# Decoded weights summed in PSUM on TensorE, and gl moved to VectorE, in an attention and two-MoE kernel

## The chip, the cores and the metric

The kernel runs on one core of one Trainium2 chip. The metric is the device time of one execution in microseconds; the time of the kernel before is the median of three runs.

## What is computed

Packed attention feeds a dense MLP, and that feeds a mixture of eight experts, of which each token takes two. Cut to what matters here:

```python
p_packed = sm_attn(p, k, v)              # 32 packed queries per head over 576 keys
x = sm_attn(q, p_packed, p_packed)       # 4608 tokens x 512
h = x @ w_in                             # 512 -> 2048
g = np.maximum(h, 0.0) ** 2
x = g @ w_out                            # 2048 -> 512
# then: noisy top-2 gate, and per expert relu(x @ w1[e]) @ w2[e], weighted and added up
```

The weights `w_in` and `w_out` are float32 to NumPy's eye, but this kernel's inputs arrive as 64-bit words (the host only views their bits), so the chip has to turn pairs of 32-bit words into float32 first. That is the decoding of which this document speaks.

## The kernel before

The kernel has two stages. In the first, the 4608 tokens go through the dense MLP in 16 blocks of 288 (block j). In the second, the eight experts each take three tiles of gathered tokens. Blocks 0 to 14 and all that they need are *units*: each unit has an engine, a cost, a list of units that must come first, and the PSUM buffers that it takes. A planner in `schedule()` simulates the engines in the order of time and emits the units in one fixed order, by priorities (`AHEAD`, in thousands of ns per kind of unit) and due times (`DUE`). Engines then run their queues strictly in that order. Block 15 and the experts are emitted by a loop written out by hand behind it.

The units are these.

- **Decoding** (`decode(n)`, 32 chunks of 128 x 512: 16 of `w_in`, 16 of `w_out`, alternating). A load; o0 on ScalarE (L206); o1 to o5 on VectorE (L210, L214, L218, L222, L226), which leave a high part in `dec_a` and a small part in `dec_t`; o6 on GpSimd adds the two (L235 into `win`, L232 into `dec_a` for `w_out`). For `w_out` ScalarE rounds the sum to fp32r as the high half of `wo` (o7, L104 by the helper `act_copy`), and VectorE subtracts it for the low half (o8, L241).
- **Part 1** (`part1(n)`, kind A): scores of packed queries (L291), softmax, transposes (L310, L312), products with v (L324), for a half of a batch's heads; two of them fill `pk[b]`.
- **Preparation** (`prepare(b, q)`, kind P): `pk[b]` times a quarter of `win` (L374), which folds `p_packed` into `w_in`; ScalarE and VectorE split the result into high and low halves in `ring` (L395).
- **Part 2** (`part2(j)`, kind Q): scores of block j's tokens against `pk`, softmax, transposed; ScalarE rounds it to `xT[j, 0]` and the difference goes to `xT[j, 1]` (L449; VectorE for blocks 0 and 1, `JA = 2`, else GpSimd).
- **MLP steps** (`moe_step(j, f)`, kind M, f from 0 to 15): six first-layer matmuls (`moe_l1`, L648) into `ph`; ScalarE's relu (L655) and square; `gh` is the rounded square and `gl` the rest (`moe_gl`, L671; VectorE for blocks 0 and 1, else GpSimd, after VectorE's square at L666); then twelve second-layer matmuls (`moe_l2`, L680) into four accumulators. Step f needs chunk f of `w_out` decoded; steps run in one chain through all blocks.
- **Routing** (`logits`, `route`, kinds R and U): gates of finished blocks, top 2, ranks, and scatters of list entries to `lst` in DRAM by GpSimd (L620), each behind the one before.

PSUM has two buffers tagged `side` (`side()`), which part 1, part 2, the preparations and the routing share. Filler matmuls on `ones` (L1103) keep TensorE going in gaps before 45 us (`WARM`). In block 15's first step the loop loads the list of the first expert and computes a group index from it on VectorE (`group_index`, L790), and the copies of block 14's accumulators to `x2T` (`moe_x2`, L687) come behind it.

Products keep close to fp32 accuracy by splitting both factors into two fp32r halves; three of the four cross terms are multiplied (`TERMS`).

Of the kernel before, what the change touches and what calls it, by code (L numbers as in the profile page):

```python
# [9 lines left out]
F = mybir.dt.float32  # L10
# [11 lines left out]
P = 128  # L22
# [20 lines left out]
for x, sl in enumerate((1, 2, 3, 4, 5, 6, 7, 9, 11, 12, 13, 14, 15, 16)):  # L43
    G0.setdefault(sl, []).append((x // 8, x % 8 // 2, 2 * (x % 2)))
QB, PKB = 2, 2
STB = 3
# [9 lines left out]
FULL = 1275  # L56
AHEAD = {"r": 38.7, "d": 21, "D": 10.3, "a": 17.1, "A": 59.2, "q": 41.7, "Q": 4.8, "p": 44.4, "P": 6.5, "R": 18.2, "M": 1.4, "w": 0.2}
DUE = 13
RING = 8
# [26 lines left out]
def program(ctx, tc, qT, kT, v, pT, w_in, w_out, wg, wn, noise, w1, w2, out):  # L86
# [86 lines left out]
    p1, c_p1 = open_pool("p1", "left")  # L173

    chunks = []
    for i in range(NFF + 4):
# [20 lines left out]
    def decode(n):  # L197
# [26 lines left out]
        def o5():  # L224
            a, t = st["a"].bitcast(F), st["t"].bitcast(F)
            nc.vector.scalar_tensor_tensor(t, raw[n][:, :, 0].bitcast(U32), 2.0 ** -52, t,  # L226
                                           op0=OP.mult, op1=OP.mult)

        def o6():
            a, t = st["a"].bitcast(F), st["t"].bitcast(F)  # L230
            if kind:
                nc.gpsimd.tensor_add(a, a, t)  # L232
            else:
                a, t = (y.rearrange("p (c f) -> p c f", c=4) for y in (a, t))
                nc.gpsimd.tensor_add(win[:, :, P * i:P * i + P], a, t)  # L235

# [3 lines left out]
        def o8():  # L240
            nc.vector.tensor_sub(wo[:, i, 1], st["a"].bitcast(F), wo[:, i, 0].bitcast(F))  # L241

        x = ("d", n)
        unit(("r", n), "sp", load, [("d", n - STB, 5)], dma=524288)
        unit(x + (0,), "act", o0, [("r", n), ("d", n - 2, 6)], 520)
        unit(x + (1,), "dve", o1, [x + (0,)], 480)
        unit(x + (2,), "dve", o2, [x + (1,)], 600)
        unit(x + (3,), "dve", o3, [x + (2,), ("d", n - TB, 6), ("d", n - TB, 8)], 950)
        unit(x + (4,), "dve", o4, [x + (3,)], 680)
        unit(x + (5,), "dve", o5, [x + (4,)], 680)  # L250
        unit(x + (6,), "pool", o6, [x + (5,)] + (lent if not kind and i >= LENT_FROM else []), 1400)
        if kind:
            unit(x + (7,), "act", o7, [x + (6,)], 600)
            unit(x + (8,), "dve", o8, [x + (7,)], 690)

# [121 lines left out]
    def prepare(b, q):  # L377
        n = 8 * b + 2 * q
        st = {}

        def u_g():
            st["m"] = [side(f"mp{r}", [P, 512]) for r in range(2)]
            heads(b, st["m"], win[:, :, 512 * q:512 * q + 512])

        def half(a, r):
            return ring[:, entry(n):entry(n) + 2, a, 256 * r:256 * r + 256]

        def u_h():
            wm[b, 2 * q], wm[b, 2 * q + 1] = piece(n), piece(n + 1)
            for r in range(2):  # L390
                act_copy(half(0, r), st["m"][r].rearrange("p (n f) -> p n f", n=2))

        def u_l():
            for r in range(2):
                nc.vector.tensor_sub(half(1, r), st["m"][r].rearrange("p (n f) -> p n f", n=2), half(0, r).bitcast(F))  # L395

        x = ("P", b, q)
        m = n - RING + 1
        old = [("M", 2 * (m // 8) + 1, 2 * (m % 8) + 1, "1")] if m >= 0 else []
        unit(x + ("g",), "pe", u_g, [("A", 2 * b, "y"), ("A", 2 * b + 1, "y")] +  # L400
             [("d", chunks.index((0, 4 * q + i)), 6) for i in range(4)] + old, 900, psum=(x + ("l",),) * 2)
        unit(x + ("h",), "act", u_h, [x + ("g",)], 1200)
        unit(x + ("l",), "dve", u_l, [x + ("h",)], 1240)
# [3 lines left out]
    def part2(j):  # L407
# [40 lines left out]
        def u_d():  # L448
            (nc.vector if j < JA else nc.gpsimd).tensor_sub(xT[j, 1], st["aT"], xT[j, 0].bitcast(F))  # L449

# [8 lines left out]
        unit(x + ("h",), "act", u_h, [x + ("t",), ("M", j - 2, NFF - 1, "1")], 620)  # L459
        unit(x + ("d",), "dve" if j < JA else "pool", u_d, [x + ("h",)], 700 if j < JA else 1600)  # L460

# [190 lines left out]
    def moe_g(j, f):  # L652
# [3 lines left out]
        gh = mo.tile([P, BLK], FR, name="gh", bufs=3)  # L656
        if j < JA:
            nc.scalar.activation(g, g, AF.Square)
# [3 lines left out]
        gs[j, f] = g, gh  # L662

    def moe_gg(j, f):
        g = gs[j, f][0]
        nc.vector.tensor_mul(g, g, g)  # L666

    def moe_gl(j, f):
        g, gh = gs[j, f]
        gl = mo.tile([P, BLK], FR, name="gl", bufs=3)  # L670
        (nc.vector if j < JA else nc.gpsimd).tensor_sub(gl, g, gh.bitcast(F))  # L671
        gs[j, f] = gh, gl
# [29 lines left out]
    def moe_step(j, f):  # L702
# [6 lines left out]
        if j < JA:  # L709
            unit(x + ("l",), "dve", lambda: moe_gl(j, f), [x + ("g",)], 400)  # L710
        else:
            unit(x + ("q",), "dve", lambda: moe_gg(j, f), [x + ("g",)], 400)
            unit(x + ("l",), "pool", lambda: moe_gl(j, f), [x + ("q",)], 850)
        if (j, f) in ((NS - 1, NFF - 1), (NS - 1, NFF - 2)):
# [194 lines left out]
    def schedule():  # L909
# [20 lines left out]
        def kind(x):  # L930
            if x[0] == "d" and x[-1] in (7, 8):
                return "w"
            if x[0] == "d":
# [375 lines left out]
```

## Time and profile before

| | |
|---|---|
| median of 3 runs | 1748.86 us (1743.95 to 1750.26) |
| the profiled execution | 1746.33 us, of which the span 1744.5 us |
| mean granted TensorE clock | 0.972 |
| TensorE busy | 1643.3 us (94%) |
| VectorE busy | 839.5 us (48%) |
| ScalarE busy | 616.2 us (35%) |
| GpSimd busy | 762.2 us (44%) |

The profile comes from one execution. Engines: PE is TensorE's matmuls, PEld its weight loads, DVE VectorE, ACT ScalarE, POOL GpSimd, SP the queue that issues most transfers. A line number is that of the kernel before; a copy by ScalarE stands at L104, the helper's line, so it is told apart by its tiles. In a window, "busy" is the time covered by at least one instruction; records of a group may overlap. PEclk is the granted TensorE clock as a share of full speed: 1.00 is 2.4 GHz and 0.50 is 1.2 GHz. In brackets behind an instruction stands the idle time before it and what ended it.

### The profile page before, as it was taken

Reading aid. Unit: us, or ns where it says so; the run is one execution under the profiler, and the core shown is the slowest. Engines: PE = TensorE matmul, PEld = TensorE weight load, DVE = VectorE, ACT = ScalarE, POOL = GpSimd, SP = SyncE. Lnnn points to the kernel's source line nnn. Section 1 sums busy time; section 2 is a strip of 40 time slices with the busy share of each in tenths; the row PEclk is TensorE's granted clock in tenths of the full one; section 3 lists DMA queues with packets and bytes.
Section 4 is the critical chain, followed back from the end, with each engine's and each line's share of the span. In section 5 each row is a group of like instructions: output and inputs, shape, how many; then the busy total and the mean of one; then the engine's idle time right before and its main releaser. Section 6 shows DMA issues by size and latency. Waiting matters only on the chain. (4 is left out here: it accounts for less than half of the span.)

```text
span 1744.5 us, 29040 instructions
## 1 busy us (share of the span) xinstructions
PE 1643.3 (94%) x11142; PEld 1432.8 (82%) x11142; DVE 839.5 (48%) x1849; ACT 616.2 (35%) x1323; POOL 762.2 (44%) x754
## 2 busy tenths in 40 slices
PE   8578999999999999996899799999999999999997
PEld 7357898889889888996778689888898888988886
DVE  7996554646464555543644444433334343433321
ACT  3455544444444444442523222322222232322211
POOL 2232153534334353525734655537355362644611
PEclk9689999999999999998999899999999999999998
DMA  8553123132323121100413534434344342534322
GB/s 252 166 151 85 42 61 101 48 89 53 110 53 93 47 74 44 29 15 17 120 38 84 116 79 92 86 74 103 70 94 88 69 112 62 111 83 84 76 26 31
DMA packets 143667, 140.82 MB, mean 81 GB/s; under 512 B 33071, under 2 KB 111919, under 8 KB 143527
## 3 DMA queue, kind: packets, MB, share of 16 engines
q1 hardware_dynamic: 120295, 100.05, 20.5%
q0 software_dynamic: 23232, 38.90, 12.9%
q8 instruction: 88, 1.44, 0.3%
q14 instruction: 52, 0.43, 0.1%
HBM read 99.71 MB, written 39.19 MB: 80 GB/s over the span
## 5 line engine op out<-in xcount | busy, mean ns | idle before, releaser
L680 PE MATMUL acc<-gh,wo 128*128 128x288 f32 x2048 | 434.5, 304 | 13.7 <-ACT wo L104 5.0
L680 PEld LDWEIGHTS acc<-gh,wo 128*128 128x128 f32 x2048 | 334.3, 192 | 42.3 <-issue 21.2
L827 POOL DMA_INDIRECT xg<-x2d,gi x296 | 295.8, 999 | 100.0 <-issue 97.6
L680 PE MATMUL acc<-gl,wo 128*128 128x288 f32 x1024 | 309.4, 302 | 26.5 <-POOL gl L671 22.9
L860 DVE SCALAR_TENSOR_TENSOR hl<-ph,hh 128x512 fp32r<-128x512 f32 (+3 forms) x184 | 105.8, 575 | 436.3 <-ACT hh L859 436.3
L671 POOL TENSOR_TENSOR gl<-g,gh 128x288 fp32r<-128x288 f32 x224 | 181.0, 810 | 284.9 <-DVE g L666 133.4
L882 POOL DMA_INDIRECT out<-y,ls x76 | 122.7, 1614 | 327.1 <-DVE y L879 160.9
L859 ACT ACTIVATE hh<-ph 128x512 fp32r<-128x512 f32 (+3 forms) x184 | 93.0, 505 | 487.0 <-PE ph L853 487.0
L648 PE MATMUL ph<-xT,ring 128*128 128x288 f32 x1536 | 243.7, 302 | 2.3 <-ACT g L655 1.3
L648 PEld LDWEIGHTS ph<-xT,ring 128*128 128x128 f32 x1536 | 217.2, 192 | 24.3 <-issue 10.5
L853 PE MATMUL ph<-ring,wb 128*128 128x512 f32 (+3 forms) x1152 | 225.4, 345 | 9.6 <-ACT ring L104 9.6
L680 PEld LDWEIGHTS acc<-gl,wo 128*128 128x128 f32 x1024 | 197.1, 193 | 33.7 <-POOL gl L671 29.7
L853 PE MATMUL ph<-ring,wo 128*128 128x512 f32 (+3 forms) x1152 | 222.9, 342 | 1.6 <-ACT ring L104 1.3
L853 PEld LDWEIGHTS ph<-ring,wb 128*128 128x128 f32 x1152 | 196.0, 189 | 34.0 <-ACT ring L104 10.1
L666 DVE TENSOR_TENSOR g<-g 128x288 f32<-128x288 f32 x224 | 129.0, 579 | 180.8 <-ACT gh L661 179.7
L853 PEld LDWEIGHTS ph<-ring,wo 128*128 128x128 f32 x1152 | 194.8, 189 | 24.7 <-ACT ring L104 1.8
L655 ACT ACTIVATE g<-ph 128x288 f32<-128x288 f32 x256 | 104.3, 407 | 266.0 <-PE ph L648 192.4
L870 PE MATMUL acc<-wo,hh 128*128 128x512 f32 (+1 forms) x608 | 191.1, 395 | 0.0
L870 PE MATMUL acc<-wb,hh 128*128 128x512 f32 (+1 forms) x576 | 179.3, 393 | 0.0
L620 POOL DMA_INDIRECT lst<-ent,pi x96 | 92.1, 960 | 121.6 <-DMA lst<-ent,pi 63.9
L870 PEld LDWEIGHTS acc<-wo,hh 128*128 128x128 f32 (+1 forms) x608 | 110.4, 185 | 22.8 <-issue 0.5
L870 PEld LDWEIGHTS acc<-wb,hh 128*128 128x128 f32 (+1 forms) x576 | 104.8, 185 | 20.7
(198 smaller groups left out, 1803.3 us busy)
## 6 DMA issues: line engine op xcount, KB each, us to landing
wst<-w SPq DMA_DIRECT2D x128, 256.0 KB, 2.8
out<-zero SPq DMA_DIRECT2D x37, 256.0 KB, 4.2
q<-qT SPq DMA_DIRECT2D x16, 576.0 KB, 4.4
x2d<-x2s SPq DMA_DIRECT2D x64, 144.0 KB, 2.9
kq<-kT SPq DMA_DIRECT2D x15, 576.0 KB, 3.8
st<-w_in SPq DMA_DIRECT2D x16, 512.0 KB, 3.8
st<-w_out SPq DMA_DIRECT2D x16, 512.0 KB, 4.5
vq<-v SPq DMA_DIRECT2D x15, 512.0 KB, 4.3
```

Source lines behind the costliest of these rows:

```text
L620: nc.gpsimd.indirect_dma_start(out=lst, out_offset=bass.IndirectOffsetOnAxis(ap=st["pi"][:, r, k:k + 1], axis=0), in_=st["ent"][:, r, k], ...
L648: nc.tensor.matmul(ph, w[:, a, d], xT[j, b][:, d], start=n == 0, stop=n == 5)
L655: nc.scalar.activation(g, ph, AF.Relu)
L666: nc.vector.tensor_mul(g, g, g)
L671: (nc.vector if j < JA else nc.gpsimd).tensor_sub(gl, g, gh.bitcast(F))
L680: nc.tensor.matmul(acc[j][d], wo[:, f, b, d * P:(d + 1) * P], g[a], start=f == 0 and n == 0, stop=f == NFF - 1 and n == 2)
L827: nc.gpsimd.indirect_dma_start(out=g[:, x], out_offset=None, in_=src, in_offset=bass.IndirectOffsetOnAxis(ap=idx, axis=0))
L853: nc.tensor.matmul(ph, wblock(e, f, a)[:, c], xt[t][b][:, c, :n], start=i == 0, stop=i == 11)
L859: nc.scalar.activation(hh, ph, AF.Relu)
L860: nc.vector.scalar_tensor_tensor(hl, ph, 0.0, hh.bitcast(F), op0=OP.max, op1=OP.subtract)
L870: nc.tensor.matmul(acc["e", t, r], h[a][:, o:o + n], wblock(e, 8 + f, b).rearrange("p c f -> p (c f)"), start=first and i == 0, stop=last ...
L882: nc.gpsimd.indirect_dma_start(out=out, out_offset=bass.IndirectOffsetOnAxis(ap=sl[:, 0:1], axis=0), in_=y, in_offset=None, compute_op=OP.add)
```

## The change

The sum of a decoded chunk moves to TensorE. o5 now writes its part as bf16 into a tile of its own (`dec_b`, two buffers). o6 is two matmuls into a `side` buffer, identity times `dec_a` in plain fp32 and a bf16 identity times `dec_b`; for `w_out` a third one, minus the identity times the high half, sits between them. ScalarE rounds `dec_a` alone to the high half (o7) and evacuates the PSUM buffer (o8) into `win` or the low half of `wo`. GpSimd's 32 additions and VectorE's 16 subtractions are gone. `gl` is always on VectorE, and for block 15 it follows a square on ScalarE, as for blocks 0 and 1. The low half of `xT` is always on GpSimd. Part 2's `q` has one buffer rather than two. The planner gets other costs, priorities and due times. The stage of the experts is not touched. The whole diff:

```diff
@@ -42,7 +42,7 @@
 G0 = {}
 for x, sl in enumerate((1, 2, 3, 4, 5, 6, 7, 9, 11, 12, 13, 14, 15, 16)):
     G0.setdefault(sl, []).append((x // 8, x % 8 // 2, 2 * (x % 2)))
-QB, PKB = 2, 2
+QB, PKB = 1, 2
 STB = 3
 NFF = FF // P
 LAG = 2
@@ -54,8 +54,8 @@
 WARM = 45000
 TICK = 10240 / 3
 FULL = 1275
-AHEAD = {"r": 38.7, "d": 21, "D": 10.3, "a": 17.1, "A": 59.2, "q": 41.7, "Q": 4.8, "p": 44.4, "P": 6.5, "R": 18.2, "M": 1.4, "w": 0.2}
-DUE = 13
+AHEAD = {"r": 76.2, "d": 20, "D": -2.5, "a": 111.6, "A": 57.6, "q": 30.5, "Q": 4.5, "p": 95.2, "P": 6.1, "R": 96.4, "M": 1.4, "s": 81.3, "S": 22.9}
+DUE = 9
 RING = 8
 JA = 2
 RP = [5, 8]
@@ -172,6 +172,10 @@
     late = {}
     p1, c_p1 = open_pool("p1", "left")
 
+    ident16 = p1.tile([P, P], BF, name="ident16")
+    nc.vector.tensor_copy(ident16, ident)
+    minus = p1.tile([P, P], FR, name="minus")
+    nc.scalar.activation(minus, ident, AF.Copy, scale=-1.0)
     chunks = []
     for i in range(NFF + 4):
         if i < NFF:
@@ -222,36 +226,39 @@
             nc.vector.tensor_scalar(st["t"], st["a"], -0x00800000, None, op0=OP.bitwise_and)
 
         def o5():
-            a, t = st["a"].bitcast(F), st["t"].bitcast(F)
-            nc.vector.scalar_tensor_tensor(t, raw[n][:, :, 0].bitcast(U32), 2.0 ** -52, t,
+            st["b"] = stg.tile([P, 512], BF, name="dec_b", bufs=2)
+            nc.vector.scalar_tensor_tensor(st["b"], raw[n][:, :, 0].bitcast(U32), 2.0 ** -52, st["t"].bitcast(F),
                                            op0=OP.mult, op1=OP.mult)
 
         def o6():
-            a, t = st["a"].bitcast(F), st["t"].bitcast(F)
+            st["s"] = side("sum", [P, 512])
+            nc.tensor.matmul(st["s"], ident, st["a"].bitcast(F), start=True, stop=False)
             if kind:
-                nc.gpsimd.tensor_add(a, a, t)
-            else:
-                a, t = (y.rearrange("p (c f) -> p c f", c=4) for y in (a, t))
-                nc.gpsimd.tensor_add(win[:, :, P * i:P * i + P], a, t)
+                nc.tensor.matmul(st["s"], minus, wo[:, i, 0], start=False, stop=False)
+            nc.tensor.matmul(st["s"], ident16, st["b"], start=False, stop=True)
 
         def o7():
             act_copy(wo[:, i, 0], st["a"].bitcast(F))
 
         def o8():
-            nc.vector.tensor_sub(wo[:, i, 1], st["a"].bitcast(F), wo[:, i, 0].bitcast(F))
+            if kind:
+                act_copy(wo[:, i, 1], st["s"])
+            else:
+                act_copy(win[:, :, P * i:P * i + P], st["s"].rearrange("p (c f) -> p c f", c=4))
 
         x = ("d", n)
         unit(("r", n), "sp", load, [("d", n - STB, 5)], dma=524288)
-        unit(x + (0,), "act", o0, [("r", n), ("d", n - 2, 6)], 520)
-        unit(x + (1,), "dve", o1, [x + (0,)], 480)
-        unit(x + (2,), "dve", o2, [x + (1,)], 600)
-        unit(x + (3,), "dve", o3, [x + (2,), ("d", n - TB, 6), ("d", n - TB, 8)], 950)
-        unit(x + (4,), "dve", o4, [x + (3,)], 680)
-        unit(x + (5,), "dve", o5, [x + (4,)], 680)
-        unit(x + (6,), "pool", o6, [x + (5,)] + (lent if not kind and i >= LENT_FROM else []), 1400)
+        unit(x + (0,), "act", o0, [("r", n), ("d", n - 2, 5)], 620)
+        unit(x + (1,), "dve", o1, [x + (0,)], 450)
+        unit(x + (2,), "dve", o2, [x + (1,)], 417)
+        unit(x + (3,), "dve", o3, [x + (2,), ("d", n - TB, 6)], 682)
+        unit(x + (4,), "dve", o4, [x + (3,)], 456)
+        unit(x + (5,), "dve", o5, [x + (4,), ("d", n - 2, 6)], 680)
         if kind:
-            unit(x + (7,), "act", o7, [x + (6,)], 600)
-            unit(x + (8,), "dve", o8, [x + (7,)], 690)
+            unit(x + (7,), "act", o7, [x + (3,)], 620)
+        unit(x + (6,), "pe", o6, [x + (5,), x + (7,)] + (lent if not kind and i >= LENT_FROM else []), 1560 if kind else 1300,
+             psum=(x + (8,),))
+        unit(x + (8,), "act", o8, [x + (6,)], 620)
 
 
     pk = {}
@@ -398,7 +405,7 @@
         m = n - RING + 1
         old = [("M", 2 * (m // 8) + 1, 2 * (m % 8) + 1, "1")] if m >= 0 else []
         unit(x + ("g",), "pe", u_g, [("A", 2 * b, "y"), ("A", 2 * b + 1, "y")] +
-             [("d", chunks.index((0, 4 * q + i)), 6) for i in range(4)] + old, 900, psum=(x + ("l",),) * 2)
+             [("d", chunks.index((0, 4 * q + i)), 8) for i in range(4)] + old, 900, psum=(x + ("l",),) * 2)
         unit(x + ("h",), "act", u_h, [x + ("g",)], 1200)
         unit(x + ("l",), "dve", u_l, [x + ("h",)], 1240)
 
@@ -446,7 +453,7 @@
             act_copy(xT[j, 0], st["aT"])
 
         def u_d():
-            (nc.vector if j < JA else nc.gpsimd).tensor_sub(xT[j, 1], st["aT"], xT[j, 0].bitcast(F))
+            nc.gpsimd.tensor_sub(xT[j, 1], st["aT"], xT[j, 0].bitcast(F))
 
         x, prev = ("Q", j), ("Q", j - 1)
         unit(x + ("l",), "sp", u_l, [("Q", j - QB, "s")], dma=393216)
@@ -457,7 +464,7 @@
         unit(x + ("n",), "dve", u_n, [x + ("e",)], 2050)
         unit(x + ("t",), "dve", u_t, [x + ("n",), prev + ("h",), prev + ("d",)], 680)
         unit(x + ("h",), "act", u_h, [x + ("t",), ("M", j - 2, NFF - 1, "1")], 620)
-        unit(x + ("d",), "dve" if j < JA else "pool", u_d, [x + ("h",)], 700 if j < JA else 1600)
+        unit(x + ("d",), "pool", u_d, [x + ("h",)], 1500)
 
 
     def count_key():
@@ -654,21 +661,25 @@
         g = mo.tile([P, BLK], F, name="g", bufs=2)
         nc.scalar.activation(g, ph, AF.Relu)
         gh = mo.tile([P, BLK], FR, name="gh", bufs=3)
-        if j < JA:
+        if long(j):
             nc.scalar.activation(g, g, AF.Square)
             act_copy(gh, g)
         else:
             nc.scalar.activation(gh, g, AF.Square)
         gs[j, f] = g, gh
 
+    def long(j):
+        return j < JA or j == NB - 1
+
     def moe_gg(j, f):
         g = gs[j, f][0]
-        nc.vector.tensor_mul(g, g, g)
+        if not long(j):
+            nc.vector.tensor_mul(g, g, g)
 
     def moe_gl(j, f):
         g, gh = gs[j, f]
         gl = mo.tile([P, BLK], FR, name="gl", bufs=3)
-        (nc.vector if j < JA else nc.gpsimd).tensor_sub(gl, g, gh.bitcast(F))
+        nc.vector.tensor_sub(gl, g, gh.bitcast(F))
         gs[j, f] = gh, gl
 
     def moe_l2(j, f):
@@ -707,10 +718,9 @@
         unit(x + ("g",), "act", lambda: moe_g(j, f), [x + ("1",), ("M",) + p[2] + ("l",), ("M",) + p[3] + ("2",)],
              1240 if j < JA else 830)
         if j < JA:
-            unit(x + ("l",), "dve", lambda: moe_gl(j, f), [x + ("g",)], 400)
+            unit(x + ("l",), "dve", lambda: moe_gl(j, f), [x + ("g",)], 450)
         else:
-            unit(x + ("q",), "dve", lambda: moe_gg(j, f), [x + ("g",)], 400)
-            unit(x + ("l",), "pool", lambda: moe_gl(j, f), [x + ("q",)], 850)
+            unit(x + ("l",), "dve", lambda: (moe_gg(j, f), moe_gl(j, f)), [x + ("g",)], 900)
         if (j, f) in ((NS - 1, NFF - 1), (NS - 1, NFF - 2)):
             return
         unit(x + ("2",), "pe", lambda: moe_l2(j, f), [x + ("l",), ("d", chunks.index((1, f)), 8), ("M",) + p[1] + ("2",)] +
@@ -928,8 +938,8 @@
         due = {x: rank.get(("M", 2 * x[1] + 3, DUE, "1"), 0) if x[0] == "U" else rank.get(("M", x[1] + 1, DUE, "1"), 0) for x in names if x[0] in "RU"}
 
         def kind(x):
-            if x[0] == "d" and x[-1] in (7, 8):
-                return "w"
+            if x[0] == "d" and x[-1] in (6, 7, 8):
+                return "sS"[chunks[x[1]][0]]
             if x[0] == "d":
                 return "dD"[chunks[x[1]][0]]
             if x[0] in "XU":
```


## Rows read from the trace of the kernel before

**Rows 1.** The page, part 1: TensorE's busy us, share of the span, instructions.

```profile
PE 1643.3 (94%) x11142; PEld 1432.8 (82%) x11142; DVE 839.5 (48%) x1849; ACT 616.2 (35%) x1323; POOL 762.2 (44%) x754
```

**Rows 2.** Groups by line, TensorE, 0 to 156 us: count | busy us, mean ns | idle.

```profile
L680 PE MATMUL acc<-gh,wo 128*128 128x288 f32 x128 | 33.3, 345 | 9.4 <-ACT wo L104 5.0 <-DVE wo L241 4.4
L1103 PE MATMUL acc<-ones 128*128 128x128 bf16 x532 | 33.0, 225 | 1.1 <-DVE warm L1096 1.1
```

**Rows 3.** Windows of 0 to 156 us: length, busy (x) PE, PEld, DVE, ACT, POOL, PEclk, DMA.

```profile
70.00:80.00 10.00, 4.92 (x24) 1.44 (x24) 9.77 (x19) 4.21 (x9) 3.83 (x3) 0.50 0.53 153
...
90.00:100.00 10.00, 10.00 (x97) 8.66 (x89) 9.35 (x21) 6.40 (x16) 2.92 (x2) 0.84 0.50 166
...
sum 156.00, PE 111.98 PEld 90.79 DVE 133.52 ACT 69.49 POOL 50.62; mean PE 6.59 PEld 5.34 DVE 7.85 ACT 4.09 POOL 2.98
```

**Rows 4.** Timeline, TensorE, 95 to 96 us: start us, us, engine, line.

```profile
95.34 0.43 PE L680 MATMUL acc<-gh,wo 128*128 128x288 f32 x2
95.61 0.29 PE L680 MATMUL acc<-gl,wo 128*128 128x288 f32 x1
95.74 0.43 PE L680 MATMUL acc<-gh,wo 128*128 128x288 f32 x2
```

**Rows 5.** Timeline, 0 to 60 us: a score, a product and a preparation.

```profile
15.86 1.19 PE L291 MATMUL s<-win,pq 128*64 128x288 f32 x8
...
26.54 0.90 PE L324 MATMUL pp<-win,a1T 128*32 128x64 f32 x40 [1.14 <-ACT a1T L104]
...
34.54 1.09 PE L374 MATMUL mp<-win,pk 64*32 64x512 f32 x16
```

**Rows 6.** Groups by line, ScalarE, 0 to 156 us: the first decode step.

```profile
L206 ACT ACTIVATE dec_t<-st 128x512 f32<-128x512 f32 x32 | 21.5, 673 | 67.8 <-POOL dec_a L232 35.5 <-DMA st<-w_in 20.6 <-POOL win L235 10.2
```

**Rows 7.** Groups by line, VectorE, 0 to 156 us.

```profile
L241 DVE TENSOR_TENSOR wo<-dec_a,wo 128x512 fp32r<-128x512 f32 x16 | 21.1, 1316 | 1.8 <-ACT wo L104 1.8
L222 DVE TENSOR_SCALAR dec_t<-dec_a 128x512 int32<-128x512 int32 x32 | 15.8, 494 | 0.1
L210 DVE TENSOR_SCALAR dec_t<-dec_t 128x512 f32<-128x512 f32 x32 | 15.7, 492 | 14.5 <-ACT dec_t L206 14.3
```

**Rows 8.** Timeline, GpSimd, one addition at 61 us.

```profile
60.88 1.38 POOL L235 TENSOR_TENSOR win<-dec_a,dec_t 128x512 f32<-128x512 f32 x1 [1.90 <-DVE dec_t L226]
```

**Rows 9.** Timeline, VectorE, 61 to 72 us.

```profile
61.05 1.76 DVE L241 TENSOR_TENSOR wo<-dec_a,wo 128x512 fp32r<-128x512 f32 x1
...
66.30 0.42 DVE L222 TENSOR_SCALAR dec_t<-dec_a 128x512 int32<-128x512 int32 x1
...
71.49 0.68 DVE L241 TENSOR_TENSOR wo<-dec_a,wo 128x512 fp32r<-128x512 f32 x1
```

**Rows 10.** Groups by line and form, 0 to 760 us: fp32 matmuls.

```profile
L374 PE MATMUL mp<-win,pk 64*32 64x512 f32 x480 | 35.3, 616 | 6.7 <-DVE ppo L333 6.7
...
L310 PE MATMUL ta<-ident,a 128*128 128x128 f32 x64 | 11.1, 297 | 6.0 <-ACT a L304 4.9 <-DVE a L422 1.1
```

**Rows 11.** The page, part 5: a 512-column fp32r group.

```profile
L870 PE MATMUL acc<-wo,hh 128*128 128x512 f32 (+1 forms) x608 | 191.1, 395 | 0.0
```

**Rows 12.** Waits of TensorE, 156 to 800 us: us in total, times, longest.

```profile
PE acc L680 <- POOL gl L671: 9.0, 10, 3.0
```

**Rows 13.** Timeline, VectorE, a gl of block 0.

```profile
80.60 0.45 DVE L671 TENSOR_TENSOR gl<-g,gh 128x288 fp32r<-128x288 f32 x1
```

**Rows 14.** Windows of 156 to 800 us, columns as in rows 3: the sum.

```profile
sum 644.00, PE 633.96 PEld 570.21 DVE 341.84 ACT 290.75 POOL 256.98; mean PE 48.77 PEld 43.86 DVE 26.30 ACT 22.37 POOL 19.77
```

**Rows 15.** Timeline, TensorE, 818 to 824 us: the wait and its releaser in brackets.

```profile
818.65 0.61 PE L680 MATMUL acc<-gl,wo 128*128 128x288 f32 x1 [8.52 <-POOL gl L671]
...
823.56 0.85 PE L680 MATMUL acc<-gh,wo 128*128 128x288 f32 x2 [4.31 <-DVE x2T L687]
```

**Rows 16.** Timeline, VectorE, the group index at 822 us.

```profile
822.55 0.23 DVE L790 TENSOR_SCALAR gi<-lg,pq 128x16 int32<-128x16 int32 x1 [15.93 <-DMA lg<-lst]
```

**Rows 17.** Waits of TensorE, 830 to 900 us.

```profile
PE acc L680 <- POOL gl L671: 4.9, 4, 2.2
```

## The prediction, made before the changed kernel was run

> **What bounds the kernel now.** I read the totals first, then the windows of the opening, then who waits for whom. TensorE is busy 94% of the span [rows 1], so a gain can only come from stretches in which it idles, runs filler or has the lower clock. The opening, to about 156 us, holds most of that. By 156 us the 192 second-layer matmuls of token block 0 have run (128 with gh, half as many with gl), and beside them 33.0 us of filler [rows 2]. The window row of 0 to 156 has TensorE busy 112.0, filler included, VectorE busy 133.5, and windows such as 70 to 80 at half clock, while 90 to 100, full of work, is back at 0.84 [rows 3]. From 156 to 800 us it is busy 634 of 644 [rows 14].
>
> How much of those 156 us was useful, at full clock? Three matmuls of 288 columns take 0.40 us from start to start, 0.133 each [rows 4]. Block 0 has 16 steps of 18, so 38 us. Five groups of part 1 cost about 3 us each (scores 1.19, products 0.90, transposes about 1), four weight preparations 1.09 each [rows 5], two part 2 scores I take as much: together some 22 more, an estimate. So about 60 of 156 us were useful and 96 were lost.
>
> What sets the pace of the opening is VectorE: it decodes 32 weight chunks, and block 0's step f can't run its second layer before output chunk f is decoded. ScalarE's first decode step waited 35.5 and 10.2 us for GpSimd's additions and 20.6 us for loads [rows 6]; it has room.
>
> **The change, part by part.** *VectorE's relief.* The 16 splits at L241, 21.1 us [rows 7], go. The 32 GpSimd additions go too, and with them what they did to VectorE: beside an addition of 1.38 us [rows 8], an L241 took 1.76 us, and alone 0.68; L222 takes 0.42 alone [rows 9]. Over 32 calls L222 and L210 stand at 0.494 and 0.492 [rows 7], so they return 32 x 0.073 twice, 4.7 us; the other decode steps return a little more, which I leave against the two xT splits that now go to GpSimd. Together 21.1 + 4.7 = 26 us. If VectorE alone bounds the opening, block 0 ends at 156 - 26 = 130.
>
> The Trainium skill (SBUF — State Buffer, Terms, "shared port pair") says that VectorE and GpSimd arbitrate for one pair of ports and that "the loser **fully blocks**" for the whole instruction. The 1.08 us between the two L241 rows fits it, but by the rule all of GpSimd's additions, 32 of roughly the length seen, some 44 us, could come back, and VectorE would be done before 110; the means show far less, so I stay with them.
>
> *TensorE's new work.* Per input chunk one plain fp32 matmul of 512 columns by ident and one bf16; per output chunk a third in fp32r. The trace has no such fp32 matmul on the full array. A 288-column record lasts 0.29 and paces 0.133 [rows 4], so 0.16 is latency. An fp32 record of 512 columns lasts 0.616, so it streams 0.45, and such a plain fp32 matmul leaves two records (480 for 30 units of eight matmuls); a 512-column fp32r record lasts 0.395 and streams 0.23 [rows 10, 11]. Input chunk: 0.90 + 0.23 = 1.13. Output chunk: 1.36. Sixteen of each: 40 us. Lower end: the transposes by ident, 297 for 128 columns [rows 10], leave one record, which would make it 0.45 + 0.23 and 0.45 + 0.46, 25 us. Upper end: nothing overlaps, 1.63 and 2.02, 58 us. I take 42, nearest to the plain fp32 row, with a little for weight loads. At half clock all of it doubles.
>
> The Trainium skill (FP8 and Floating Point Precision, "TensorE Precision Notes") gives true FP32 as four passes through the array, which speaks against sums by fp32 identity. Against one pass that streams 0.23 us it would make 0.92 us for the ident matmul, the two-record reading rather than the one-record one.
>
> *The opening's sum.* Need up to the end of block 0: 60 + 42 = 102 us of TensorE. Until 45 us fillers run because nothing is ready; two part 1 groups, a preparation and some eight sums fit there, about 18. Then 84 us are left, from 45 on: at best 129, as late as VectorE's 130. Two engines that must both be full do not both stay full. Before, about 52 of the 60 useful us fell between 45 and 156, so that stretch lost 59; I give the new one 13 us of gaps and lower clock (a fifth to a quarter, since the sums fill TensorE's gaps). Block 0 ends at 142: 14 us gained, between 26 (no loss) and -10 (loss of 37).
>
> New waits: VectorE's last decode step (o5) now waits for the TensorE sum two chunks back, because dec_b has two buffers. Behind it in VectorE's queue lie the next decode steps and block 0's gl, for which TensorE waits. The sums also take the two PSUM buffers tagged side, which part 1, part 2 and the preparations use. ScalarE gets 32 evacuations of about 0.67 [rows 6], 21 us on 69.5 of 156 [rows 3]; at 90 of 142 it hides them. Part 2's q on one buffer costs nothing: it is loaded once per block, 16 x 2.4 = 38 us of TensorE. Identity copies cost under 1 us at the start.
>
> *gl on VectorE, blocks 2 to 14.* TensorE waited 9.0 us for GpSimd's gl here [rows 12], mostly with list scatters in GpSimd's queue. VectorE needs about 0.45 for a gl [rows 13], so 13 x 16 x 0.45 = 94 us on 342 of 644 [rows 14], 68%. It fits, and a hop between engines goes. Where a gl now falls behind a long VectorE step (a block transpose, routing) TensorE waits in turn: I give back 3 of the 9. Net -6, between -9 and +9.
>
> *The hand-over, 800 to 900 us.* TensorE waited 8.52 us for a gl of block 15, then 4.31 for a copy of block 14's sums [rows 15]. The gl lay in GpSimd's queue behind paced list scatters; the copy lay in VectorE's queue behind the group index at L790, which had waited 15.93 us for the list [rows 16]. Moving gl frees the first wait, but TensorE only reaches the second sooner: the copy still comes when the list has landed. So of 12.8 only what the scatters finish earlier comes back; GpSimd free of gl and routing with a higher priority (18.2 to 96.4) should bring some 3 us. The later waits for GpSimd's gl, 4.9 us [rows 17], go. So -8, between 0 and -14. ScalarE's third instruction per step of block 15 is hidden: three short instructions in a step of 18 x 0.133 = 2.4 us.
>
> The expert stage is untouched. **Sum:** profiled execution 1746.33 - 14 - 6 - 8 = 1718.3. The median of the runs lies 2.5 us above that execution, so 1720.8; I say 1720.
>
> **The rivals.** (1) *TensorE becomes the bound of the opening.* If the sums arrive spread out, the clock stays at half as it was at 70 to 80 [rows 3]. Half rate from 45 to 100 does 27 of the 84 us; the other 57 at three quarters of the speed need 76 and end at 176 to 179. That loses 20 to 23, less 14 won later: 1748.9 + 22 - 14 = 1757. It makes the kernel slower at all from the point where block 0 ends past 170. For it: those half-clock windows. Against: the window that was full of work had its clock back, and ready work is plenty. Chance 0.08.
> (2) *The wait is only exchanged.* Every sum holds a side buffer from its first matmul to the end of ScalarE's copy, some 2.3 us (an estimate: 1.13 to 1.36, 0.67 and two hops), and VectorE waits for it. Then the opening gains nothing: 1748.9 - 14 = 1735. For it: two buffers for everything. Against: 32 x 2.3 over two buffers is 37 us of 156. Chance 0.16.
> (3) *gl is late on VectorE.* VectorE runs in order, so routing and block transposes stand before gl; if every block loses about 1 us where it won half, the middle gives +12 and the time is 1721 + 18 = 1739. Against: VectorE at 68%. Chance 0.10.
> (4) *VectorE alone bounds the opening* at 130 and the hand-over gives 12: 1700. Chance 0.06.
>
> **How the numbers follow.** The forecast, block 0 ending between 132 and 152 and the rest as summed, has 0.60 and gives 1707 to 1734. A measurement can tell about 0.5% from no change, 8.7 us, so faster means below 1740. Faster: 0.60, rival 4 0.06, most of rival 2 0.12, half of rival 3 0.05: 0.83. Same: the rest of 2 and 3 and a little of 1: 0.10. Slower: 0.07. The range leaves out rival 1 and the ends of rivals 3 and 4: 1701 to 1744.
>
> **What would show it.** The second layer of block 0 ends near 142 rather than 156; VectorE's decode steps stand at 0.42 and 0.68 throughout; the ident matmul has two records of about 0.6 at full clock; between 156 and 800 no wait on a GpSimd gl and few on VectorE; near 810 one wait on the copy of x2T of about 9 us, with L790 before it. It is wrong if TensorE's windows from 45 to 130 stay at half clock, if VectorE waits for the sum, or if block 0 ends after 152.

## The result, and the profile after

The changed kernel takes 1715.95 us (median, 1713.52 to 1717.89) beside 1746.78 us for the kernel before: a ratio of 0.9826, 95% interval [0.9802, 0.9849], 31 us faster. The forecast was 1720, in a range of 1701 to 1744.

Where the time went is read with one mark in both traces: the start of the second copy of a block's sums to `x2T` on VectorE, which ends the block. For block 0, before and then after (timeline of VectorE):

```profile
158.65 0.45 DVE L687 COPY x2T<-acc 128x288 f32<-128x288 f32 x1
...
137.03 0.45 DVE L698 COPY x2T<-acc 128x288 f32<-128x288 f32 x1
```

Block 0 ends at 159 us before and at 137 after, block 13 at 765 and 736, block 15 at 883 and 851, the span at 1744.5 and 1711.7. So the opening gave 22 us, blocks 1 to 13 took 599 rather than 606 (7), blocks 14 and 15 took 115 rather than 118 (3), and the rest 861 rather than 862 (1). A second profile of the changed kernel, of 1716.0 us, has block 0 end at 139 and gives 20, 7, 1 and 0 in the same order: a term of this list is good to about 2 us.

The page of the kernel after, part 1 (engine, busy us, share, instructions), against [rows 1]:

```profile
PE 1650.4 (96%) x11110; PEld 1430.0 (84%) x11110; DVE 877.4 (51%) x2040; ACT 640.9 (37%) x1372; POOL 537.0 (31%) x500
```

GpSimd lost 225 us of work, TensorE's grew by 7 in a span that is 33 shorter. Windows of the opening, the kernel before and then after, columns as in [rows 3] (length, busy of PE, PEld, DVE, ACT and POOL, granted clock, DMA share, GB/s):

```profile
45.00:159.00 114.00, 75.88 (x558) 57.91 (x555) 101.50 (x194) 57.35 (x126) 39.45 (x27) 0.78 0.49 143
sum 159.00, PE 114.98 PEld 93.00 DVE 135.37 ACT 71.09 POOL 50.62; mean PE 57.49 PEld 46.50 DVE 67.68 ACT 35.54 POOL 25.31
```

```profile
70.00:80.00 10.00, 9.90 (x53) 7.08 (x52) 9.10 (x20) 8.23 (x17) 0.00 (x0) 1.00 0.57 173
...
45.00:137.00 92.00, 87.82 (x605) 61.09 (x602) 77.45 (x164) 66.21 (x142) 4.12 (x4) 1.00 0.56 162
sum 137.00, PE 127.31 PEld 90.61 DVE 109.33 ACT 84.76 POOL 5.56; mean PE 63.65 PEld 45.31 DVE 54.66 ACT 42.38 POOL 2.78
```

From 45 us to the end of block 0 TensorE was idle for 38 us of 114 and had a clock of 0.78; now it is idle for 4 of 92 and has the full clock (2.4 GHz). Window 70 to 80, at half clock before, is at 1.00. What TensorE does up to 137 us, and VectorE's decode steps (groups by line: count | busy, mean ns | idle, and what ended it), against [rows 2] and [rows 7]:

```profile
L235 PE MATMUL sum<-dec_a,ident 128*128 128x512 f32 x64 | 33.7, 608 | 2.4 <-DVE ring L402 1.5 <-ACT a L311 0.7 <-ACT wo L104 0.2
L691 PE MATMUL acc<-gh,wo 128*128 128x288 f32 x128 | 27.5, 308 | 0.0
L1113 PE MATMUL acc<-ones 128*128 128x128 bf16 x388 | 25.6, 228 | 1.1 <-DVE ones L122 1.1
...
L237 PE MATMUL sum<-wo,minus 128*128 128x512 f32 x16 | 12.7, 795 | 0.0
L238 PE MATMUL sum<-dec_b,ident 128*128 128x512 bf16 x32 | 12.3, 385 | 0.6 <-DVE dec_b L230 0.6
```

```profile
L230 DVE SCALAR_TENSOR_TENSOR dec_b<-st,dec_t 128x512 bf16<-128x512 uint32 x32 | 23.1, 726 | 0.6
L222 DVE SCALAR_TENSOR_TENSOR dec_a<-st,dec_t 128x512 int32<-128x512 int32 x32 | 21.9, 688 | 0.7
L226 DVE TENSOR_SCALAR dec_t<-dec_a 128x512 int32<-128x512 int32 x32 | 14.7, 461 | 0.3
L214 DVE TENSOR_SCALAR dec_t<-dec_t 128x512 f32<-128x512 f32 x32 | 13.6, 424 | 11.8 <-ACT dec_t L210 11.6
```

The 128 matmuls with gh, which waited 9.4 us for the decoded weights, wait for none. ScalarE's first decode step no longer waits for GpSimd, but mostly for loads [rows 6]:

```profile
L210 ACT ACTIVATE dec_t<-st 128x512 f32<-128x512 f32 x32 | 21.6, 674 | 28.1 <-DMA st<-w_in 19.1 <-DMA st<-w_out 3.7 <-DVE dec_b L230 2.9
```

Blocks 1 to 13, one window row of the kernel before and one of after, then TensorE's wait for gl in the latter (line, what it waited for: us, times, longest), against [rows 12] and [rows 14]:

```profile
160.00:765.00 605.00, 595.52 (x5146) 535.45 (x5144) 313.11 (x807) 271.96 (x651) 241.33 (x277) 1.00 0.23 63
```

```profile
137.00:736.00 599.00, 595.72 (x5215) 537.59 (x5214) 377.31 (x1011) 276.86 (x661) 87.39 (x85) 1.00 0.24 67
```

```profile
PE acc L691 <- DVE gl L682: 1.5, 3, 0.7
```

TensorE's work is the same and its idle time fell from 9.5 to 3.3 us. The hand-over, the timeline of TensorE, VectorE, SyncE's queue and GpSimd (start, us, instruction, idle before it and its releaser), against [rows 15] and [rows 16]:

```profile
797.49 0.85 PE L691 MATMUL acc<-gh,wo 128*128 128x288 f32 x2 [17.61 <-DVE x2T L698]
...
796.47 0.23 DVE L800 TENSOR_SCALAR gi<-lg,pq 128x16 int32<-128x16 int32 x1 [19.89 <-DMA lg<-lst]
...
792.89 2.25 SPq L794 DMA_DIRECT2D lg<-lst  x4
795.32 1.84 SPq L788 DMA_DIRECT2D ls<-lst  x4
797.41 0.97 SPq L763 DMA_DIRECT2D wst<-w  x2
...
761.87 0.92 POOL L627 DMA_INDIRECT lst<-ent,pi  x1 [56.92 <-DVE pi L606]
790.83 0.92 POOL L627 DMA_INDIRECT lst<-ent,pi  x1 [1.40 <-DMA lst<-ent,pi]
```

GpSimd's 12 list scatters run from 762 to 792, the list loads follow, VectorE stands 19.9 us at the group index, and behind it lies the copy for which TensorE waits 17.6 us. Before, the waits there were 8.5 and 4.3. Of GpSimd's gl in block 15 [rows 17] no wait is left.

### The profile page after: what moved, and what is told of

Read it like the earlier page. It is cut to its first block, busy times and chain, and to the rows that moved or that the text cites. A ratio compares the mean times of both kernels' runs of the same rounds, so it can differ in the third digit from the quotient of the medians.

```text
span 1711.7 us, 28563 instructions
## 1 busy us (share of the span) xinstructions
PE 1650.4 (96%) x11110; PEld 1430.0 (84%) x11110; DVE 877.4 (51%) x2040; ACT 640.9 (37%) x1372; POOL 537.0 (31%) x500
## 5 line engine op out<-in xcount | busy, mean ns | idle before, releaser
L691 PE MATMUL acc<-gh,wo 128*128 128x288 f32 x2048 | 426.1, 301 | 17.6 <-DVE x2T L698 17.6
L691 PEld LDWEIGHTS acc<-gh,wo 128*128 128x128 f32 x2048 | 330.0, 190 | 49.3 <-issue 22.4
L691 PE MATMUL acc<-gl,wo 128*128 128x288 f32 x1024 | 303.3, 296 | 1.6 <-DVE gl L682 1.5
L677 DVE TENSOR_TENSOR g<-g 128x288 f32<-128x288 f32 x208 | 98.2, 472 | 129.3 <-ACT gh L668 128.9
L682 DVE TENSOR_TENSOR gl<-g,gh 128x288 fp32r<-128x288 f32 x256 | 123.4, 482 | 51.5 <-ACT gh L104 35.7
```

The costliest lines, as they stand in the source:

```text
L682: nc.vector.tensor_sub(gl, g, gh.bitcast(F))
L691: nc.tensor.matmul(acc[j][d], wo[:, f, b, d * P:(d + 1) * P], g[a], start=f == 0 and n == 0, stop=f == NFF - 1 and n == 2)
```

## The experiments

The theory: the opening gained because VectorE lost 26 us of work and GpSimd's additions left its path, and both it and TensorE now run almost full; the middle's gain belongs to gl; the hand-over is set by the list. Rivals: the new priorities alone made the opening; one of the two engines alone bounds it; gl's place changed the hand-over. The small edits (one buffer for `q`, all low halves of `xT` on GpSimd) have no run of their own.

**gl alone.** The kernel before, with one edit:

```diff
-        (nc.vector if j < JA else nc.gpsimd).tensor_sub(gl, g, gh.bitcast(F))
+        nc.vector.tensor_sub(gl, g, gh.bitcast(F))
...
-            unit(x + ("q",), "dve", lambda: moe_gg(j, f), [x + ("g",)], 400)
-            unit(x + ("l",), "pool", lambda: moe_gl(j, f), [x + ("q",)], 850)
+            unit(x + ("l",), "dve", lambda: (moe_gg(j, f), moe_gl(j, f)), [x + ("g",)], 900)
```

> The kernel before with gl on VectorE for all blocks and nothing else of the change. If the parts add up, the opening stays as it was (block 0 ends near 156 us), the 9.0 us of waits for a GpSimd gl between 156 and 800 us and the 4.9 us in block 15 go, and the time falls by 8 to 14 us, to 1733 to 1739. Rival, that VectorE needs the relief of the sums first or that its own queue is late instead: 1745 to 1750.

1756.58 us, ratio 1.0009 [0.9987, 1.0031]. The middle was some 11 us shorter, but block 15 took 71 us, with stops of TensorE that nothing in the trace releases, such as (timeline)

```profile
832.12 0.29 PE L680 MATMUL acc<-gh,wo 128*128 128x288 f32 x1 [1.54 <-issue]
```

So it was measured again on another chip:

> The kernel before with the second rounding of the hidden values on VectorE, again, since the first time its runs lay wide apart and block 15 showed stops of TensorE that no wait explains. If the middle's gain is the rounding's own and the stops belonged to that execution, blocks 1 to 13 take some 598 us (606 before), block 15 59 and the ratio is 0.994 to 0.997. If VectorE pays the middle's gain back at the hand-over, it is 1.00 again, with waits of TensorE for VectorE in blocks 14 and 15 worth about 8 us.

1737.59 us, ratio 0.9935 [0.9919, 0.9951], and no such stops. Block 0 ends at 159, the middle takes 597, blocks 14 and 15 116. TensorE's waits there:

```profile
PE acc L680 <- DVE x2T L687: 14.7, 1, 14.7
```

So gl alone gives 11 us, 9 of them in the middle. At the hand-over the waits for GpSimd are gone and a wait of 14.7 us for the list has taken their place. Why the first chip showed the stops is not known; the two intervals don't overlap, so a single comparison on one chip can be off by 0.7%, and the second pair below by 1.0%.

**The sums alone.** The changed kernel with gl of blocks 2 to 15 back on GpSimd (and its square on VectorE in block 15):

```diff
-        nc.vector.tensor_sub(gl, g, gh.bitcast(F))
+        (nc.vector if j < JA else nc.gpsimd).tensor_sub(gl, g, gh.bitcast(F))
```

> The changed kernel with gl back on GpSimd for blocks 2 to 15 (as before), all else changed. If the parts add up, block 0 ends near 135 us as in the changed kernel, some 9 us of waits for GpSimd's gl come back in the middle, and the time is 1722 to 1730. Rival, that freeing GpSimd is what matters: over 1735.

1738.94 us, 0.9909 [0.9893, 0.9926]: above the range that was expected and, taken as a time, in that of the rival. But this run and the next are from the chip that showed the stops, where the kernel before takes 1754.75 us. They have no such stops, yet their expert stage, which no edit touches, takes 867 and 870 us rather than 862, so the ratio and the marks are what can be compared. By the ratio it is 16 us faster than the kernel before, by the marks up to the end of block 15 it is 13. Block 0 ends at 138, as with the whole change; the middle takes 612 and TensorE waits for GpSimd's gl again (block 0's end to block 15's; the kernel before has 22.9 us there):

```profile
PE acc L691 <- POOL gl L682: 25.8, 20, 9.1
```

By ratio the sums, with their priorities, give 16 us and gl 11; the whole gives 31. Where the other 4 belong isn't shown. The opening's gain doesn't need gl off GpSimd: block 0 ends at 138 without that.

**The priorities alone**, on the kernel before (`AHEAD`, `DUE` of the changed one; the weights' rounding gets 22.9):

```diff
-AHEAD = {"r": 38.7, "d": 21, "D": 10.3, "a": 17.1, "A": 59.2, "q": 41.7, "Q": 4.8, "p": 44.4, "P": 6.5, "R": 18.2, "M": 1.4, "w": 0.2}
-DUE = 13
+AHEAD = {"r": 76.2, "d": 20, "D": -2.5, "a": 111.6, "A": 57.6, "q": 30.5, "Q": 4.5, "p": 95.2, "P": 6.1, "R": 96.4, "M": 1.4, "w": 22.9}
+DUE = 9
```

> The kernel before with the changed kernel's priorities and due time in the planner, and nothing else. My theory, that the engines' work made the gain: VectorE still has its 16 subtractions and the port, block 0 ends at 150 us or later, time 1740 to 1755. Rival, that the order of the work made it: block 0 ends before 145 us and the time is below 1735.

1768.29 us, 1.009 [1.0066, 1.0114]: slower by 0.9%. Block 0 ends at 180. Blocks 1 to 13 then take 596 rather than 606, though GpSimd's gl is still waited for (11.7 us): TensorE is busy 583 us in them rather than 596, since more of their work lies in front of the mark. So with another order, a later end of block 0 is in part work done earlier, and the ratio says what the order costs. TensorE waits for ScalarE's rounding, and that for GpSimd's addition (waits, 45 to 180 us):

```profile
PE acc L680 <- ACT wo L104: 19.7, 5, 7.1
...
ACT wo L104 <- POOL dec_a L232: 26.3, 9, 6.1
```

**The sums with the old priorities**: the changed kernel with `AHEAD` and `DUE` of before, `"s": 21, "S": 0.2`.

> The changed kernel with the priorities and due time of before (sums as decode steps, evacuations and the high half as the old low-half steps). My theory: two thirds of the opening's gain remain, block 0 ends between 134 and 145 us, time 1716 to 1730. Rival, the order made it: block 0 ends after 150 us, time over 1735.

1752.99 us, 0.9992 [0.9976, 1.0009], on the chip that showed the stops, which stood here too (9.7 us of them in blocks 14 and 15). Again, on the other chip:

> The changed kernel with the priorities of the kernel before, again, for the same reason: the first time block 15 took 73 us with stops that no wait explains. If those belonged to that execution, block 0 ends at about 151 and block 15 takes 55 to 60, for a ratio near 0.992. If the old priorities themselves make block 15 longer, by weight work that comes due in it, the ratio is 1.00 again and block 15 takes over 70 us.

1729.43 us, 0.9888 [0.9867, 0.9908], and no such stops. Block 0 ends at 152, so a third of the opening's gain is left and not two thirds, as was expected; the rival's sign, an end after 150, came true, its time over 1735 did not. The window up to block 0's first copy, at 149:

```profile
45.00:149.00 104.00, 90.65 (x601) 60.15 (x603) 79.66 (x169) 63.83 (x135) 4.11 (x4) 0.90 0.47 138
```

TensorE is idle for 13 of 104 us, and the clock is 0.90. So the new order is worth some 12 us beside the sums (0.9821 for the changed kernel on this chip, below) and costs some 16 without them (from the chip of the stops, so this size is less sure, but 1% less would still leave no gain): it is no gain of its own, it spends what the sums made free. The sums without it give 20 of the 31 us.

**More work on TensorE.** The changed kernel, its first sum matmul issued twice:

```diff
             nc.tensor.matmul(st["s"], ident, st["a"].bitcast(F), start=True, stop=False)
+            nc.tensor.matmul(st["s"], ident, st["a"].bitcast(F), start=True, stop=True)
```

> The changed kernel with the identity matmul on dec_a done twice, same result: 32 x 0.9 = 29 us more of TensorE before block 0 ends, in the same order. If TensorE bounds the changed opening (its windows from 45 us on are 83 to 100% busy), block 0 ends 22 to 29 us later and the time is 1738 to 1746. If VectorE bounds it, less than 10 us, below 1726.

1736.41 us, 0.9936 [0.9917, 0.9955]. Block 0 ends at 157, 20 us later.

**More work on VectorE.** Step o4 three times instead of once:

```diff
-            nc.vector.tensor_scalar(st["t"], st["a"], -0x00800000, None, op0=OP.bitwise_and)
+            for _ in range(3):
+                nc.vector.tensor_scalar(st["t"], st["a"], -0x00800000, None, op0=OP.bitwise_and)
```

> The changed kernel with decode step o4 (mask) done three times, same result: 32 x 2 x 0.34 = 22 us more of VectorE before block 0 ends. If TensorE alone bounds the opening, VectorE's 10 us of idle time between 45 and 128 us take some of it and the time rises by 5 to 12, 1721 to 1728. If VectorE bounds it, by 18 to 22, 1734 to 1738.

1734.22 us, 0.9921 [0.9905, 0.9938]. Block 0 ends at 155, 18 us later.

**GpSimd's additions back, as mere noise**: 32 additions of 128x512, emitted behind o5, whose result nobody reads. They wait for `dec_a` alone, which o3 writes, and so mostly run beside o4 or the step behind it.

```diff
+            nc.gpsimd.tensor_add(junk, st["a"].bitcast(F), junk)
```

> The changed kernel with a GpSimd addition of 128x512 beside each chunk's last decode step, its result unused: the additions of before without the 16 subtractions. If what GpSimd's instructions did to VectorE was worth about 15 us of VectorE's time (10 on L241, 5 on others, by the rows of before), the decode steps on VectorE lengthen again by 8 to 20 us in sum and the time rises by 4 to 14, 1720 to 1730. If the meeting of the two is harmless, it stays at 1714 to 1718. If each addition stops VectorE for its whole length, 32 x 1.4 = 44 us, the time rises by 25 or more.

1733.78 us, 0.9919 [0.9902, 0.9935]. Block 0 ends at 155, 18 us later, though no engine waits for the additions. The windows of these three from 45 us on, in this order, then two groups by line of the third, up to 156 us:

```profile
45.00:156.00 111.00, 109.62 (x685) 72.43 (x688) 79.75 (x166) 68.02 (x141) 4.16 (x4) 1.00 0.47 136
```

```profile
45.00:156.00 111.00, 95.28 (x633) 65.80 (x637) 101.14 (x222) 68.59 (x143) 4.40 (x4) 0.97 0.47 136
```

```profile
45.00:156.00 111.00, 94.84 (x630) 64.72 (x633) 100.60 (x171) 68.81 (x144) 38.08 (x28) 0.97 0.48 136
```

```profile
L228 DVE TENSOR_SCALAR dec_t<-dec_a 128x512 int32<-128x512 int32 x32 | 28.9, 903 | 0.3
L234 POOL TENSOR_TENSOR junk<-dec_a,junk 128x512 f32<-128x512 f32 x32 | 44.9, 1404 | 83.1 <-DVE dec_a L224 80.5 <-DVE sm L340 2.5
```

22 us more of TensorE's work after 45 us, or 23 to 24 more of VectorE's, cost 18 to 20 each, or 16 to 18 beside the second profile of the changed kernel, with block 0's end at 139. The run on TensorE came out just under what was forecast for TensorE as the bound, the one on VectorE near what was forecast for VectorE, and the third above its forecast of 4 to 14 us. Neither engine alone bounds the opening: both lie on the path. In the third, o4 takes 903 ns rather than 461; with the other steps (L216 583 rather than 424, L232 807 rather than 726, L220 453 rather than 423, gl 609 rather than 454 over 18) that is 32 x 0.71 + 18 x 0.155 = 25.5 us: one addition of 1.40 us costs VectorE 0.80.

That mean hides two cases, which the third's timeline shows (GpSimd's additions and VectorE's instruction beside each):

```profile
60.82 1.36 POOL L234 TENSOR_TENSOR junk<-dec_a,junk 128x512 f32<-128x512 f32 x1 [3.12 <-DVE dec_a L224]
60.96 1.51 DVE L228 TENSOR_SCALAR dec_t<-dec_a 128x512 int32<-128x512 int32 x1
...
66.36 3.02 POOL L234 TENSOR_TENSOR junk<-dec_a,junk 128x512 f32<-128x512 f32 x2 [4.17 <-DVE dec_a L224]
68.17 1.27 DVE L405 TENSOR_TENSOR ring<-mp,ring 128x512 fp32r<-128x512 f32 x2
```

The o4 that begins under an addition ends 0.28 us after it, at 62.47, and so do all 15 that begin under one; alone it takes 0.42. Two splits of `ring`, whose input `mp` lies in PSUM, run beside another addition at their usual length, 0.67 each. In the kernel before, 10 of the 16 splits at L241 and 14 of the 160 decode steps began under an addition and ended 0.28 to 0.55 us behind it.

**The group index away from VectorE.** The first expert's index on GpSimd, so that the copy of `x2T` has nothing to stand behind:

```diff
-                    group_index(gi0[:, groups(k)], lg0[:, groups(k), 0])
+                    group_index(gi0[:, groups(k)], lg0[:, groups(k), 0], nc.gpsimd)
```

> The changed kernel with the first expert's group index computed on GpSimd, which waits for it anyway, and not on VectorE. If the 17.6 us wait of TensorE near 797 us is VectorE's queue standing behind that index, the wait falls below 9 us (the transposes of gathered rows become the next thing that waits), and the time falls by 5 to 12, to 1704 to 1711. If the list itself is what TensorE lacks there, the wait moves to the gathered rows and the time stays at 1713 to 1718.

1719.7 us, 0.9845 [0.9829, 0.9862]: no gain. Block 14 ends at 780, 17 us earlier, and then TensorE and ScalarE stand still (waits, 735 to 855 and 770 to 825):

```profile
PE lg L491 <- ACT lT L104: 16.2, 1, 16.2
...
ACT wo L104 <- DMA wst<-w: 24.9, 2, 19.5
```

ScalarE waits for a weight block of the first expert, whose load stands in SyncE's queue behind the load of the list (timeline of SyncE):

```profile
793.60 2.25 SPq L794 DMA_DIRECT2D lg<-lst  x4
796.03 1.84 SPq L788 DMA_DIRECT2D ls<-lst  x4
798.12 0.97 SPq L763 DMA_DIRECT2D wst<-w  x2
```

**The list's loads off SyncE too.** As the last one, and the two loads issued by GpSimd, behind the scatters that they wait for:

```diff
-                    load_groups(k, expert(0), lg0[:, groups(k)].unsqueeze(1))
+                    load_groups(k, bass.ds(reg["p"], 1), lg0[:, groups(k)].unsqueeze(1), nc.gpsimd)
...
-                    load_list(k, expert(0), ls0.unsqueeze(1))
+                    load_list(k, bass.ds(reg["p"], 1), ls0.unsqueeze(1), nc.gpsimd)
```

> The changed kernel with the first expert's list taken off the two in-order queues that the last two runs showed to stand behind it: the group index on GpSimd and the two loads of the list (lg, ls) issued by GpSimd behind the scatters they wait for, so that SyncE's loads of the first expert's weights don't stand behind them. If the hand-over's wait is head-of-line waiting in VectorE's and SyncE's queues, both the wait of TensorE for x2T (17.6 us at 797) and the one for lg <- lT (16.2 us at 802) are gone, and blocks 14 and 15 together take about 100 us rather than 115: some 1,701 us, a ratio to the kernel before near 0.974. If the list itself is what the hand-over needs (its gathers and transposes feed the first tile), the wait moves to the gathered rows and the ratio stays at 0.982.

and, on the same chip, the changed kernel itself:

> The changed kernel itself, beside the others of this chip: a ratio of 0.980 to 0.985 to the kernel before. No theory differs on it; it is what the others here are held against.

1713.81 us, 0.9795 [0.9776, 0.9814], beside 1717.42 us, 0.9821 [0.9802, 0.9841] for the changed kernel: 3.6 us less rather than 14, and the intervals overlap. Both waits are gone, but block 15 ends at 850 rather than 854, 4 us earlier and not 14. TensorE's longest waits from 785 to 850 us, then VectorE's transpose in the timeline, then two windows:

```profile
PE ph L863 <- ACT g L662: 6.5, 1, 6.5
PE rk L577 <- DVE os L571: 5.2, 1, 5.2
PE ph L655 <- ACT g L662: 4.0, 2, 2.7
```

```profile
837.23 0.71 DVE L845 STREAM_TRANSPOSE xs<-xg 128x512 f32<-128x512 f32 x1 [6.71 <-DMA xg<-x2d,gi]
```

```profile
800.00:820.00 20.00, 12.06 (x62) 11.28 (x62) 9.53 (x41) 8.87 (x20) 13.54 (x19) 0.75 0.25 67
820.00:850.00 30.00, 23.45 (x130) 21.60 (x129) 13.95 (x28) 13.38 (x30) 21.54 (x27) 0.83 0.39 91
```

VectorE now waits for the gathered rows of the first tile, ScalarE's copy waits for its transpose, and behind that copy lies a relu of block 15. The list was needed after all, a step later: TensorE is idle for 14 of the 50 us from 800 on. The clock there, 0.75 and 0.83, is also lower than the changed kernel's beside it (0.86 from 799 to 820, 0.90 from 820 to 854); how much of what the waits gave went to it, no run separates.

## Why the prediction held, and where it didn't

**VectorE's relief**, forecast at 26 us, was 26.0: busy until block 0's end 135.4 before and 109.3 after. The splits are 21.1 of it. o1 came back to 424 ns as read, o4 only to 461 and not to 420; that the total agrees to a tenth is luck, since the two windows also differ by a gl, some softmax steps of part 1 and the two `xT` splits.

**TensorE's need**, forecast at 102 us, was 127.3 less 25.6 of filler, 101.7, and the matmuls of the sums cover 43.1 us of it, where 42 were forecast. The plain fp32 matmul was the dear one of the two readings: it leaves two records (64 for 32 calls), and where it is issued twice, the second begins 0.86 us after the first in 23 of 32 pairs and 0.91 to 0.96 in the others (0.90 forecast). One group of that run (timeline):

```profile
71.01 1.02 PE L235 MATMUL sum<-dec_a,ident 128*128 128x512 f32 x2
71.87 1.02 PE L236 MATMUL sum<-dec_a,ident 128*128 128x512 f32 x2
72.73 0.38 PE L239 MATMUL sum<-dec_b,ident 128*128 128x512 bf16 x1
72.94 1.02 PE L235 MATMUL sum<-dec_a,ident 128*128 128x512 f32 x2
```

The Trainium skill gives true FP32 as four passes through the array (FP8 and Floating Point Precision, "TensorE Precision Notes"). The rows agree with it: the bf16 matmul of 512 columns takes 0.216 us to the next one's start, and four times that, an estimate, is 0.86.

**The loss of 13 us after 45 us is the term that was mis-sized**: it was 4 (92.0 less 87.8), or 6 in the second profile. It was taken as a fifth of an old loss, on the reason that two engines which must both be full don't both stay full. But the old loss was idle time and low clock together, and the sums filled the idle time: every window is at 1.00. In the prediction's own measure, the last second-layer matmul of block 0, the opening went from 155.7 to 134.1: 22 us gained, 14 forecast. That the order decides over such a term, the runs with the old priorities show: there block 0 ends at 152, with 13 us idle and a clock of 0.90. A loss taken from before can't tell which order the planner will find.

**GpSimd's additions.** The 4.7 us for their effect on the other decode steps was right in size for this kernel (over 32 calls the means of the five steps fell by some 4 us in all), but not as a price of an addition: placed as in the run with GpSimd's additions back, 32 of them cost VectorE 25.5 us. The Trainium skill says that the loser of the port pair "**fully blocks**" (SBUF — State Buffer, Terms). Single rows agree with it: the o4 at 60.96 in that run ends only after the addition. The prediction set this rule aside because the means showed far less than all 44 us; but the means were small because only 14 of the 160 steps began under an addition. The rest of an addition is paid where such a step begins under it, and the splits of `ring` paid nothing, so the price of an addition depends on what stands beside it.

**The middle**, forecast at -6, gave 7, and the runs with gl alone (-9) and with the sums alone (+6, GpSimd's waits back) put it down to gl. TensorE's waits for a gl from VectorE came to 1.5 us only.

**The hand-over**, forecast at -8, gave 3. The later waits went, as forecast: block 15 takes 54 us rather than 59. What failed is the step "GpSimd free of gl and routing with a higher priority should bring some 3 us". The first scatter comes 25.9 us after block 13's end rather than 23.3: the new order puts block 13's `lp` matmul 6.5 us behind that end rather than 4.4. And the scatters' own pace didn't change, 2.3 us from one to the next, so an emptier GpSimd had nothing to give. The wait that was forecast at about 9 us was 17.6; the rival "only exchanged", set up for the opening, came true here. In the opening it did not: VectorE's o5, which it has waiting for the sums, stood idle for 0.6 us in all (L230 above).

**The sum**: -22, -7, -3 and -1 make the 33 us between the two spans; forecast were -14, -6, -8 and 0, which make 28. Two errors of 8 and 5 us had opposite signs, so it is luck that the total is better than its terms.

**The rivals.** TensorE at half clock did not come about, though its need was as large as forecast: the work was ready. VectorE alone does not bound the opening, and gl is not late on VectorE (1.5 us).

## What to carry to other kernels

Work moved onto the busiest engine can be free where that engine stands idle in just that stretch, if the work is ready in time: cost it stage by stage, and expect the gain only together with an order that uses it. A wait at the head of an in-order queue belongs to whatever is late, not to the queue: taken from VectorE it stood on ScalarE through SyncE's queue, and then on the gathered rows; price the next late thing before taking a wait away. Before a loss of a stretch is scaled to its new length, split it into idle time, work at a lower clock and filler, since a change can remove one of them whole.

## What was not expected of the hardware

A GpSimd addition whose result nobody reads delays the path through VectorE alone: o4 at 903 ns on average with it, 461 without, and 16 to 18 us later at the end of block 0. An o4 that begins under it waits for its end; a split that reads PSUM doesn't. The granted clock from 45 us to the end of block 0 was 0.78 before, 0.90 with the sums under the old priorities and 1.00 after, although the sums add work to TensorE. After the 17.6 us wait of the hand-over the changed kernel's clock was 0.58 from 797 to 805 us, so such a wait costs more than its length. On one chip, two kernels showed stops of TensorE in block 15 that no wait explains (some 10 us), and on another the same kernels showed none; what they were stays open.
